# Four weight remainders and the gates of four chunks move to GpSimd in a scan and mixture-of-experts kernel

## The chip, the cores and the metric

The kernel runs on one core of a Trainium2 chip. The metric is the device time of one execution in microseconds (us). The core has five engines with queues of their own: TensorE (PE in the rows; PEld is its weight load), VectorE (DVE), ScalarE (ACT), GpSimd (POOL), and SyncE (SP), which only issues transfers. Each engine takes its instructions in the order in which they were written to its queue, and waits on semaphores of the others.

## The reference

```python
sig = 1.0 / (1.0 + np.exp(-f_logit))          # x, f_logit: 2 x 5056 x 256
f = lower_bound + (1.0 - lower_bound) * sig   # the gate
for t in range(S):
    h = f[:, t] * h + (1.0 - f[:, t]) * x[:, t]
    y[:, t] = h
# two layers over the 10112 tokens of y, 8 experts, w1 256 x 1024, w2 1024 x 256
expert_idx = np.argmax(logits, axis=1)        # layer 0: cosine / tau; layer 1: x @ w_gate
gate_w = probs[np.arange(N), expert_idx]      # softmax of the logits
for e in range(8):
    xe = x[expert_idx == e]
    out[expert_idx == e] = gate_w * (np.maximum(xe @ w1[e], 0.0) @ w2[e])
```

## The kernel before

**The scan.** The tokens come in 40 chunks of 256. For one chunk the inputs are loaded to the tile xf, ScalarE takes a tanh (L495), the gate is made of it by a multiplication and an addition with two columns fa and fb, 256 elements at a time, so twice for a chunk (p_gate, L501 on ScalarE, L212 on GpSimd or VectorE). VectorE then makes the scan's input (one step over 512 elements, L207, from p_scan) and runs two scans (L529). Some chunks later TensorE transposes the result (tile yt, L578 and L580), the row for each token is built (tiles row), the router picks an expert, matmuls into RK count the tokens of each expert (rank_mm L466, L468; rank_up L473, L475), and GpSimd writes the rows to their expert's place in memory with indirect DMAs (X<-row, L714), 128 tokens each.

**Layer 0.** A unit is one tile of 128 sorted tokens with one half of the hidden width. Its tokens are read transposed (xT<-X, issued by SP at L837), TensorE makes the hidden values (hps, L880, 24 matmuls), ScalarE and VectorE make of them an fp16 pair (hT: ScalarE at L893 the rounded part, VectorE at L207 the remainder), and TensorE multiplies by the second weights (ops, L912, 12 matmuls). For the first eight tiles, all with the first half come first (units 0 to 7; ScalarE keeps their partial sums in acc, L916), then the same tiles with the second half (units 8 to 15). Both hps and ops are taken from one set of PSUM buffers, in turn.

**Weights.** Every weight is held as 64 times its value in two fp16 parts: ScalarE writes the rounded part (w_hi, L410), and the remainder is 64 times the source less the rounded part (w_lo). The remainder is one VectorE step over 1024 elements (L207; W<-W,W or W<-ws,W in the rows). For the second half of layer 0 there are 16 such pieces: e 0 to 7 of the first weights (written (0, e) in the diff) and e 0 to 7 of the second weights ((1, e)). The sources of the first weights lie in the tile that later takes the second weights; those of the second weights go through three load buffers (ws), which ScalarE's queue fills again (ws<-w2a) when remainder and rounded part are made. Units 8 and on need all of them.

**Order.** A plan of numbered steps calls these parts; up to step 17 only SP's queue has an order written out, and a scheduler with its own simulated clock orders the others, so a change of cost or engine can move neighbours as well. A remainder can be put behind an instruction already issued (behind in wstep), which is an order only, no data. In the pieces below W_0_ and W_1_ are the first and second half; 102 and 103 are the first weights, 104 and 105 the second ones.

Of the kernel before, what the change touches and what calls it, by code (L numbers as in the profile page):

```python
# [32 lines left out]
 'w0': 10,  # L33
 'wstep0': 0.85,
 'early': 4,
 'gact': (4, 16),
 'urgent': ('scan', 'mm', 'sq', 'pow', 'hi', 'norm', 'top', 'rank', 'rec', 'exp', 'slot', 'up', 'gat', 'put', 'cp'),
 'gdve': 0,
 'wpe': (2, 6, 9, 12),
# [38 lines left out]
        'done': (12, 57)},  # L78
 'hiv': (2,),
 'y1': 'V',  # L80
 'wg': (0, 0, 0, 0),
 'whv': 0,
 'spto': -6,
 'sc': (0, 26),
# [60 lines left out]
def scan_moe_moe_kernel(ctx, tc, xf, emb, cst, tmp, w1a, w2a, w1b, w2b, out, seq, cfg=CFG):  # L145
# [57 lines left out]
    V, A, G, T, SP = nc.vector, nc.scalar, nc.gpsimd, nc.tensor, nc.sync  # L203

    def stt(eng, out, in0, s, in1, op0, op1, **kw):
        assert eng is V
        return eng.scalar_tensor_tensor(out=out, in0=in0, scalar=s, in1=in1, op0=op0, op1=op1, **kw)  # L207

    def ts(eng, out, in0, s1, s2, op0, op1=None):
        if op1 is None:  # L210
            return eng.tensor_scalar(out=out, in0=in0, scalar1=s1, scalar2=None, op0=op0)  # L211
        return eng.tensor_scalar(out=out, in0=in0, scalar1=s1, scalar2=s2, op0=op0, op1=op1)  # L212

    def tt(eng, out, in0, in1, op):
        return eng.tensor_tensor(out=out, in0=in0, in1=in1, op=op)
# [66 lines left out]
    wg = const.tile([P, 2, 2, E], F16, name="wg")  # L282
# [105 lines left out]
    def w_load(item):  # L388
        m, which, h, e = item
        k = 8 * which + e  # L390
        if (m, h) == (0, 0) and k < 8 + cfg["wal"]:
            t = W1[1][:, k % 8].rearrange("p k b f -> p (k b f)").bitcast(F32)
        elif (m, which, h) == (0, 0, 1):
            t = W2[1][:, e].rearrange("p k b d -> p (k b d)").bitcast(F32)
        else:
            t = st.tile([P, 1024], F32, name="ws", tag="ws")
        hwq().dma_start(out=t, in_=wsrc[m][which][:, h, e, :])
        return t

    def w_parts(item, t):  # L400
        m, which, h, e = item
        W = (W2 if which else W1)[h]
        return t.rearrange("p (k f) -> p k f", k=4 if which else 2), W[:, e, :, 0, :], W[:, e, :, 1, :]

    def w_hi(item, t):
        src, hi, lo = w_parts(item, t)
        if item[1] * 8 + item[3] < cfg["whv"] and (item[0], item[2]) == (0, 0):
            ts(V, hi, src, 64.0, None, ALU.mult)
        else:
            A.activation(out=hi, in_=src, func=ACTF.Copy, scale=64.0)  # L410

    def w_lo(item, t):
        src, hi, lo = w_parts(item, t)
        m, which, h, e = item
        k = cfg["wg"][2 * m + h]
        i = 8 * which + e
        on_g = k and (i * k) // 16 != ((i + 1) * k) // 16
        if on_g:
            ts(G, src, src, 64.0, None, ALU.mult)
            tt(G, lo, src, hi, ALU.subtract)  # L420
        else:
            stt(V, lo, src, 64.0, hi, ALU.mult, ALU.subtract)
# [17 lines left out]
    def w_sub(item, t):  # L440

        src, hi, lo = w_parts(item, t)
        k = src.shape[1] // 2
        ps = []
        for i in range(2):
            d = pb.tile([P, 2, 256], F32, name="wd", tag="b").rearrange("p a b -> p (a b)").rearrange("p (k f) -> p k f", k=k)
            T.matmul(out=d, lhsT=idt, rhs=src[:, i * k:(i + 1) * k], start=True, stop=False)
            T.matmul(out=d, lhsT=idn, rhs=hi[:, i * k:(i + 1) * k], start=False, stop=True)
            ps.append(d)
        return ps  # L450

    def w_sub2(item, ps, t):
        src, hi, lo = w_parts(item, t)
        k = src.shape[1] // 2
        for i in range(2):
            A.activation(out=lo[:, i * k:(i + 1) * k], in_=ps[i], func=ACTF.Copy, scale=64.0)
# [269 lines left out]
    tablast = []  # L726
# [492 lines left out]
    def behind(item, eng, other=None):  # L1219
        m, which, h, e = item  # L1220
        if (m, h) == (0, 1):
            u = 2 + e // 2 if which else (e - 2) // 2
            if eng is A and u > 0:
                u -= 1
            if u >= 0:
                other = evs[u][eng is V]
        return tc.issue_after(other) if other is not None else ExitStack()

    def wstep(load, hi, lo, lo2):
        def w_done(item):  # L1230
            assert item[0] or item[2] or now[0] <= 0, "weights too late"
            wdone.add(item)

        if lo2 in wps:
            w_sub2(lo2, *wps.pop(lo2))
            w_done(lo2)
        if lo is not None:
            t = wbuf.pop(lo)
            nlo[0] += 1
            i = nlo[0]  # L1240
            if i in cfg["wpe"]:
                wps[lo] = (w_sub(lo, t), t)
            elif 16 < i <= 32 and tablast:
                with behind(lo, V, tablast[0]):
                    w_lo(lo, t)
                w_done(lo)
            else:
                w_lo(lo, t)
                w_done(lo)
        if hi is not None:  # L1250
            with behind(hi, A):
                w_hi(hi, wbuf[hi])
        if load is not None:
            wbuf[load] = w_load(load)

    def wplan(items, start, step, ahead=0, staged=0):
        x = start

        def it(k):
            return items[k] if 0 <= k < len(items) else None  # L1260

        if ahead:
            for k in range(len(items)):
                at(max(first - 2, int(start + (k - ahead) * step)), cfg["wlp"], wstep, it(k), None, None, None)
        for k in range(len(items) + 4):
            at(int(x), cfg["wprio"], wstep, None if ahead or k < staged else it(k), it(k - 2), it(k - 3), it(k - 4))
            x += step
# [7 lines left out]
    for e in range(E):  # L1275
        at(int(first + cfg["w1s"][0] + e * cfg["w1s"][1]), 60, wstep, (0, 0, 1, e), None, None, None)
# [125 lines left out]
    with ExitStack() as region:  # L1402
# [6 lines left out]
        i = first - 2  # L1409
# [117 lines left out]
```

## Time and profile before

| what | value |
|---|---|
| three runs | 1043.24, 1048.29, 1054.22 us |
| median | 1048.29 us |
| profiled execution | 1049.57 us |
| its span, first to last instruction | 1047.8 us |
[...]
| busy: TensorE, VectorE, ScalarE, GpSimd | 983.6, 780.0, 516.2, 428.2 us |

Durations and starts of single instructions come from the one profiled execution; the median says how fast the kernel usually is. A busy share is a mean over stages that differ, so it has to be read together with the stretches.

### The profile page before, as it was taken

How to read it: one execution, taken by the hardware profiler on the slowest of the kernel's cores; microseconds unless marked ns; L12 is line 12 of the kernel's file. 1: busy time of each engine (PE TensorE's matmuls, PEld its weight loads, DVE VectorE, ACT ScalarE, POOL GpSimd, SP SyncE). 2: the span in 40 equal slices, each digit the busy share in tenths (PEclk: the TensorE clock that was granted, in tenths of full speed). 3: DMA queues.
4: the chain of work that ended last, by engine and by line, in shares of the span. 5: the costliest groups of instructions: out<-in, count | busy, mean ns of one | idle time of the engine just before them, and what ended most of it. 6: DMA issues, size and time to landing. Idle time of an engine off the chain costs nothing.

```text
span 1047.8 us, 33840 instructions
## 1 busy us (share of the span) xinstructions
PE 983.6 (94%) x11795; PEld 859.2 (82%) x11795; DVE 780.0 (74%) x2288; ACT 516.2 (49%) x1266; POOL 428.2 (41%) x686
## 2 busy tenths in 40 slices
PE   5647999998999999999999999999999999999997
PEld 4436899897999899999999888998777777777775
DVE  7878797787888786765448877447777777777775
ACT  6867666555655554665345565443333333333332
POOL 5642447665666565432003550243222222222223
PEclk9967999999999999999999999999999999999999
DMA  9797545887888785965379699652222222221220
GB/s 355 244 328 170 158 93 136 155 163 135 166 161 157 141 150 104 203 200 147 60 181 208 112 212 245 116 104 72 52 52 52 52 52 51 46 52 45 47 47 31
DMA packets 216964, 137.64 MB, mean 131 GB/s; under 512 B 190961, under 2 KB 193918, under 8 KB 216800
## 3 DMA queue, kind: packets, MB, share of 16 engines
q1 hardware_dynamic: 192736, 61.63, 32.1%
q10 hardware_dynamic: 12208, 42.29, 14.7%
q0 software_dynamic: 11856, 31.51, 10.4%
q8 instruction: 105, 1.72, 0.7%
q14 instruction: 59, 0.48, 0.2%
HBM read 58.89 MB, written 38.85 MB: 93 GB/s over the span
## 4 chain that ended last, share of the span: by engine, by line
PE 49%; DMA 3%; DVE 2%; issue 1%; ACT 1%; POOL 0%; ACTq 0%; POOLq 0%
PE hps L869 10%; PE ops L908 10%; PE ops L912 9%; PE hps L880 9%; PE hps L870 5%; PE ops L909 5%; DMA X<-trow,tsl 2%; DMA xT<-X 1%; DVE hT L207 1%; DVE trow L207 0%; DVE W L207 0%; DVE trow L211 0%; PE x2p L978 0%; ACT hT L893 0%; ACT trow L935 0%
## 5 line engine op out<-in xcount | busy, mean ns | idle before, releaser
L880 PE MATMUL hps<-xT,W 128*128 128x128 f16 x4992 | 318.8, 220 | 15.3 <-DMA xT<-X 11.6
L880 PEld LDWEIGHTS <-W 128*128 x4992 | 299.0, 98 | 22.5 <-DMA xT<-X 11.8
L912 PE MATMUL ops<-W,hT 128*128 x2496 | 310.7, 274 | 3.3 <-ACT acc L916 2.7
L912 PEld LDWEIGHTS <-hT 128*128 128x128 f16 x2496 | 234.9, 98 | 31.2 <-issue 4.2
L891 DVE TENSOR_REDUCE acc<-hps 128x256 f32<-128x512 f32 x248 | 169.9, 687 | 63.5 <-PE hps L870 63.5
L207 DVE SCALAR_TENSOR_TENSOR hT<-hps,hT 128x512 f16<-128x512 f32 x208 | 142.0, 686 | 88.7 <-ACT hT L893 87.8
L1083 POOL DMA_INDIRECT out<-osum,ti x83 | 81.1, 977 | 268.7 <-DVE acc L891 227.3
L893 ACT ACTIVATE hT<-acc 128x512 f16<-128x512 f32 x124 | 78.1, 630 | 222.6 <-DVE acc L891 222.6
L893 ACT ACTIVATE hT<-hps 128x512 f16<-128x512 f32 x208 | 123.2, 592 | 116.5 <-PE hps L880 103.1
L869 PE MATMUL hps<-xT,W 128*128 128x256 f16 x992 | 177.1, 273 | 0.0
L870 PE MATMUL hps<-xT,W 128*128 128x128 f16 x992 | 170.4, 219 | 0.0
L908 PE MATMUL ops<-W,hT 128*128 x496 | 167.8, 379 | 0.0
L909 PE MATMUL ops<-W,hT 128*128 x496 | 135.2, 273 | 0.0
L1058 POOL DMA_INDIRECT X<-trow,tsl x83 | 91.8, 1106 | 67.9 <-issue 23.6
L869 PEld LDWEIGHTS <-W 128*128 x992 | 97.1, 98 | 24.1
L714 POOL DMA_INDIRECT X<-row,sl x79 | 90.3, 1143 | 57.3 <-ACT hT L893 19.4
L870 PEld LDWEIGHTS <-W 128*128 x992 | 97.1, 98 | 1.4
L207 DVE SCALAR_TENSOR_TENSOR hT<-acc,hT 128x512 f16<-128x512 f32 x124 | 84.5, 682 | 2.2 <-ACT hT L893 2.2
L908 PEld LDWEIGHTS <-hT 128*128 128x128 f16 x496 | 48.5, 98 | 45.6
L950 ACT ACTIVATE trow<-osum,tsc 128x256 f16<-128x256 f32 x62 | 28.2, 501 | 60.4 <-DVE tsc L212 57.1
L909 PEld LDWEIGHTS <-hT 128*128 128x128 f16 x496 | 48.5, 98 | 4.3
L207 DVE SCALAR_TENSOR_TENSOR W<-ws,W 128x1024 f16<-128x1024 f32 x35 | 42.6, 1221 | 11.8 <-ACT W L410 11.5
(170 smaller groups left out, 1297.1 us busy)
## 6 DMA issues: line engine op xcount, KB each, us to landing
xf<-xf ACTq DMA_DIRECT2D x27, 512.0 KB
ws<-w1b ACTq DMA_DIRECT2D x16, 512.0 KB
ws<-w2b ACTq DMA_DIRECT2D x16, 512.0 KB
W<-w1a SPq DMA_DIRECT2D x11, 512.0 KB
W<-xf SPq DMA_DIRECT2D x8, 512.0 KB
ws<-w2a ACTq DMA_DIRECT2D x8, 512.0 KB
WD<-wq SPq DMA_DIRECT2D x8, 512.0 KB
W<-WD ACTq DMA_DIRECT2D x8, 512.0 KB
```

What stands on the lines that cost most here:

```text
L207: return eng.scalar_tensor_tensor(out=out, in0=in0, scalar=s, in1=in1, op0=op0, op1=op1, **kw)
L714: w = G.indirect_dma_start(out=X[0], out_offset=IndirectOffsetOnAxis(ap=p["sl"][:, i, 0:1], axis=0), in_=p["row"][:, i, :].bitcast(I32), i ...
L869: T.matmul(out=hps[:, c % 2], lhsT=w[2 * k], rhs=xt[:, k:k + 3:2, :], start=(k == 0), stop=False)
L870: T.matmul(out=hps[:, c % 2, 0], lhsT=w[2 * k + 1], rhs=xt[:, k, :], start=False, stop=(k == 1))
L880: T.matmul(out=hps[:, c, :], lhsT=w, rhs=xt[:, a, :], start=(n == 0), stop=(n == 5))
L891: V.tensor_reduce(out=s[:, 2 * c:2 * c + 2].unsqueeze(3), in_=x.rearrange("p c b q -> p c q b"), axis=AX.X, op=ALU.add)
L893: i = A.activation(out=hh[:, 0], in_=hps, func=ACTF.Relu)
L908: T.matmul(out=t["o"].rearrange("p b d -> p (b d)"), lhsT=hT[:, k, :], rhs=w, start=(first and k == 0), stop=False)
L909: T.matmul(out=o, lhsT=hT[:, 4 + k, :], rhs=w[:, 0:D], start=False, stop=(last and k == 3))
L912: T.matmul(out=o, lhsT=hT[:, a + k, :], rhs=w[:, b * D:(b + 1) * D], start=(first and k == 0 and n == 0), stop=(last and k == 3 and n == 2))
L1058: x_write(1, G.indirect_dma_start(out=X[1], out_offset=IndirectOffsetOnAxis(ap=sl[:, i, 0:1], axis=0), in_=d["row"][:, i].bitcast(I32), in ...
L1083: i = ins_of(G.indirect_dma_start(out=out, out_offset=IndirectOffsetOnAxis(ap=ti, axis=0), in_=r, in_offset=None, bounds_check=N - 1, oob_ ...
```

## The change

The gates of chunks 12 to 15 are made by GpSimd in place of ScalarE. Four of the 16 remainders of layer 0's second half are made by GpSimd in two steps, a product with 64 in place over the source and a subtraction of the rounded part, in place of one VectorE step; these four are also not put behind an instruction of VectorE. The old switch wg, which was off everywhere, is gone. Lines after L415 have a number that is smaller by 3 in the new kernel.

```diff
--- before.py
+++ after.py
@@ -33,7 +33,7 @@
  'w0': 10,
  'wstep0': 0.85,
  'early': 4,
- 'gact': (4, 16),
+ 'gact': (4, 12),
  'urgent': ('scan', 'mm', 'sq', 'pow', 'hi', 'norm', 'top', 'rank', 'rec', 'exp', 'slot', 'up', 'gat', 'put', 'cp'),
  'gdve': 0,
  'wpe': (2, 6, 9, 12),
@@ -78,7 +78,7 @@
         'done': (12, 57)},
  'hiv': (2,),
  'y1': 'V',
- 'wg': (0, 0, 0, 0),
+ 'wgs': ((0, 4), (0, 7), (1, 2), (1, 4)),
  'whv': 0,
  'spto': -6,
  'sc': (0, 26),
@@ -412,10 +412,7 @@
     def w_lo(item, t):
         src, hi, lo = w_parts(item, t)
         m, which, h, e = item
-        k = cfg["wg"][2 * m + h]
-        i = 8 * which + e
-        on_g = k and (i * k) // 16 != ((i + 1) * k) // 16
-        if on_g:
+        if (m, h) == (0, 1) and (which, e) in cfg["wgs"]:
             ts(G, src, src, 64.0, None, ALU.mult)
             tt(G, lo, src, hi, ALU.subtract)
         else:
@@ -1241,7 +1238,7 @@
             if i in cfg["wpe"]:
                 wps[lo] = (w_sub(lo, t), t)
             elif 16 < i <= 32 and tablast:
-                with behind(lo, V, tablast[0]):
+                with behind(lo, V, tablast[0]) if (lo[1], lo[3]) not in cfg["wgs"] else ExitStack():
                     w_lo(lo, t)
                 w_done(lo)
             else:
```

GpSimd, from the four indirect writes of chunks 8 and 9 on, before. (inv and ri are small steps of the routers; row<-cs copies token numbers; xf is a gate; the second gate shown here is chunk 16's.)

```order
L714 DMA X_99<-row,sl 82048x258 x4
L212 TENSOR_SCALAR inv<-exr 128x2 x2
L700 COPY row<-cs 128x4
L215 TENSOR_TENSOR ri<-ss,hf 128x4
L211 TENSOR_SCALAR ri<-ri 128x4
L212 TENSOR_SCALAR xf<-xf,fa,fb 128x256 x2
L700 COPY row<-cs 128x4
L215 TENSOR_TENSOR ri<-ss,hf 128x4
L211 TENSOR_SCALAR ri<-ri 128x4
L714 DMA X_99<-row,sl 82048x258 x4
```

The same engine and place, after:

```order
L711 DMA X_99<-row,sl 82048x258 x4
L212 TENSOR_SCALAR xf<-xf,fa,fb 128x256 x2
L212 TENSOR_SCALAR inv<-exr 128x2 x2
L211 TENSOR_SCALAR W_1_105<-W_1_105 128x1024
L697 COPY row<-cs 128x4
L211 TENSOR_SCALAR W_1_105<-W_1_105 128x1024
L215 TENSOR_TENSOR W_1_103<-W_1_105,W_1_103 128x2x512
L211 TENSOR_SCALAR ws<-ws 128x1024
L215 TENSOR_TENSOR W_1_103<-W_1_105,W_1_103 128x2x512
L212 TENSOR_SCALAR xf<-xf,fa,fb 128x256 x4
L215 TENSOR_TENSOR ri<-ss,hf 128x4
L215 TENSOR_TENSOR W_1_105<-ws,W_1_105 128x4x256
```

Chunk 12's two gates now stand right behind the writes. Three products, two subtractions and the gates of chunks 13 and 14 stand ahead of the first small step ri, and more follow.

VectorE, from the input of chunk 12 (xf, 128x512) and its scans on, before:

```order
L207 SCALAR_TENSOR_TENSOR xf<-xf 128x512
L529 SCALAR_TENSOR_TENSOR xf<-xf 128x256 x2
L207 SCALAR_TENSOR_TENSOR hT<-hps,hT 128x512
L207 SCALAR_TENSOR_TENSOR W_1_103<-W_1_105,W_1_103 128x2x512 x2
L207 SCALAR_TENSOR_TENSOR hT<-hps,hT 128x512
L207 SCALAR_TENSOR_TENSOR W_1_103<-W_1_105,W_1_103 128x2x512 x2
L207 SCALAR_TENSOR_TENSOR hT<-hps,hT 128x512
L207 SCALAR_TENSOR_TENSOR W_1_103<-W_1_105,W_1_103 128x2x512 x2
L207 SCALAR_TENSOR_TENSOR W_1_105<-ws,W_1_105 128x4x256 x2
L212 TENSOR_SCALAR pi<-ss 128x2
L207 SCALAR_TENSOR_TENSOR hT<-hps,hT 128x512
```

The same engine and place, after:

```order
L207 SCALAR_TENSOR_TENSOR xf<-xf 128x512
L526 SCALAR_TENSOR_TENSOR xf<-xf 128x256 x2
L207 SCALAR_TENSOR_TENSOR hT<-hps,hT 128x512
L207 SCALAR_TENSOR_TENSOR W_1_103<-W_1_105,W_1_103 128x2x512 x2
L207 SCALAR_TENSOR_TENSOR hT<-hps,hT 128x512
L207 SCALAR_TENSOR_TENSOR W_1_103<-W_1_105,W_1_103 128x2x512
L207 SCALAR_TENSOR_TENSOR hT<-hps,hT 128x512
L207 SCALAR_TENSOR_TENSOR W_1_103<-W_1_105,W_1_103 128x2x512
L207 SCALAR_TENSOR_TENSOR W_1_105<-ws,W_1_105 128x4x256 x2
L212 TENSOR_SCALAR pi<-ss 128x2
L207 SCALAR_TENSOR_TENSOR hT<-hps,hT 128x512 x2
```

The input and the scans of chunk 12 have kept their place ahead of the steps hT of units 0 to 4, and two of the remainders between these are gone.

TensorE, at the second group of rank matmuls (tri16b) of chunks 10 and 11, before. It stands behind the second matmul of unit 5 (ops) and ahead of unit 9's hps:

```order
L912 MATMUL ops<-W_0_104,hT 128x256
L473 LDWEIGHTS tri16b
L473 MATMUL RK<-oh,tri16b 128x32
L475 LDWEIGHTS ones_109
L475 MATMUL RK<-oh,ones_109 128x24
L475 LDWEIGHTS ones_109
L475 MATMUL RK<-oh,ones_109 128x16
L475 LDWEIGHTS ones_109
L475 MATMUL RK<-oh,ones_109 128x8
L811 REGISTER_ALU
L880 LDWEIGHTS W_1_103
L880 MATMUL hps<-xT,W_1_103 128x128
```

The same group of rank matmuls, after; the rows ahead of it are unit 7's hps, and those behind it the second matmul of unit 4:

```order
L877 MATMUL hps<-xT,W_0_102 128x128
L470 LDWEIGHTS tri16b
L470 MATMUL RK<-oh,tri16b 128x32
L472 LDWEIGHTS ones_109
L472 MATMUL RK<-oh,ones_109 128x24
L472 LDWEIGHTS ones_109
L472 MATMUL RK<-oh,ones_109 128x16
L472 LDWEIGHTS ones_109
L472 MATMUL RK<-oh,ones_109 128x8
L909 LDWEIGHTS hT
L808 REGISTER_ALU
L909 MATMUL ops<-W_0_104,hT 128x256
```

The group has moved ahead by more than one unit, so that the second matmuls of units 4 and 5 now stand behind it.

## Rows read from the trace of the kernel before

**Rows 1.** The page, busy time of TensorE, its share of the span and its instructions.
```profile
PE 983.6 (94%) x11795; PEld 859.2 (82%) x11795; DVE 780.0 (74%) x2288; ACT 516.2 (49%) x1266; POOL 428.2 (41%) x686
```

**Rows 2.** Stretches of 10 us: busy us (instructions) by engine, clock, DMA share, GB/s.
```profile
80.00:90.00 10.00, 5.22 (x55) 4.50 (x54) 8.83 (x10) 8.75 (x17) 3.00 (x4) 0.83 0.94 170
90.00:100.00 10.00, 7.84 (x61) 6.97 (x59) 6.79 (x14) 6.89 (x17) 1.43 (x2) 0.66 0.66 180
...
120.00:130.00 10.00, 9.85 (x117) 8.90 (x117) 6.40 (x36) 5.86 (x22) 7.80 (x10) 1.00 0.74 186
```

**Rows 3.** Timeline of TensorE: start, us, line, operation, [idle before <-releaser].
```profile
82.28 1.59 PE L912 MATMUL ops<-W,hT 128*128 x12
88.56 2.74 PE L880 MATMUL hps<-xT,W 128*128 128x128 f16 x24 [4.70 <-DMA xT<-X]
...
93.41 2.72 PE L912 MATMUL ops<-W,hT 128*128 x12
...
100.31 2.72 PE L912 MATMUL ops<-W,hT 128*128 x12 [2.47 <-ACT acc L916]
...
107.36 1.86 PE L880 MATMUL hps<-xT,W 128*128 128x128 f16 x24
109.08 1.56 PE L912 MATMUL ops<-W,hT 128*128 x12
...
147.83 1.39 PE L880 MATMUL hps<-xT,W 128*128 128x128 f16 x22
```

**Rows 4.** Timeline of VectorE from 76 to 92 us.
```profile
76.69 0.69 DVE L207 SCALAR_TENSOR_TENSOR xf<-xf 128x512 f32<-128x512 f32 x1 [1.07 <-ACT xf L501]
...
85.70 0.69 DVE L207 SCALAR_TENSOR_TENSOR hT<-hps,hT 128x512 f16<-128x512 f32 x1 [1.17 <-ACT hT L893]
...
90.91 0.68 DVE L207 SCALAR_TENSOR_TENSOR hT<-hps,hT 128x512 f16<-128x512 f32 x1
```

**Rows 5.** Timeline of GpSimd from 79 to 120 us.
```profile
79.89 1.48 POOL L714 DMA_INDIRECT X<-row,sl  x1 [0.30 <-issue]
...
113.77 1.45 POOL L212 TENSOR_SCALAR xf<-xf,fa,fb 128x256 f32<-128x256 f32 x2 [16.89 <-ACT xf L495]
...
118.11 1.42 POOL L714 DMA_INDIRECT X<-row,sl  x1 [0.72 <-DVE mx L648]
```

**Rows 6.** Timeline of ScalarE from 75 to 101 us; ACTq is its DMA queue.
```profile
75.56 1.09 ACT L501 ACTIVATE xf<-xf,fb,fa 128x256 f32<-128x256 f32 x2
...
93.66 0.33 ACTq L397 DMA_DIRECT2D ws<-w2a  x1
...
97.26 1.06 ACT L410 ACTIVATE W<-ws 128x1024 f16<-128x1024 f32 x1 [1.92 <-DMA ws<-w2a]
...
99.88 0.38 ACT L916 ACTIVATE acc<-ops 128x256 f32<-128x256 f32 x1
```

**Rows 7.** Groups by shape: count | busy us, mean ns of one | idle before, releasers.
```profile
L212 POOL TENSOR_SCALAR xf<-xf,fa,fb 128x256 f32<-128x256 f32 x46 | 25.7, 565 | 37.5 <-ACT xf L495 37.5
...
L212 POOL TENSOR_SCALAR inv<-exr 128x2 f32<-128x2 f32 x41 | 12.4, 302 | 3.2 <-DMA exr<-X 0.3
L215 POOL TENSOR_TENSOR tsh<-tsh,lf 128x16 f32<-128x16 f32 x41 | 10.5, 256 | 5.5 <-DVE ter L207 3.0 <-DVE tse L1036 0.9
L215 POOL TENSOR_TENSOR lf<-exr,us 128x2 f32<-128x2 f32 x41 | 9.3, 226 | 93.1 <-DVE us L211 51.6 <-DVE tm L1015 17.1 <-DVE tse L207 16.3
L215 POOL TENSOR_TENSOR trow<-tse,lf 128x2 f32<-128x2 f32 x41 | 8.9, 216 | 19.3 <-DVE tse L1040 14.3 <-DVEq L1380 3.2 <-DVE tmx L1006 0.6
...
L207 DVE SCALAR_TENSOR_TENSOR W<-ws,W 128x1024 f16<-128x1024 f32 x35 | 42.6, 1221 | 11.8 <-ACT W L410 11.5
```

**Rows 8.** Timelines of GpSimd (POOL) and VectorE (DVE) where both work.
```profile
12.86 2.42 POOL L212 TENSOR_SCALAR W<-W,fa,fb 128x256 f32<-128x256 f32 x2
...
113.89 0.96 DVE L529 TENSOR_TENSOR_SCAN xf<-xf 128x256 f32<-128x256 f32 x1
...
115.32 0.74 DVE L529 TENSOR_TENSOR_SCAN xf<-xf 128x256 f32<-128x256 f32 x1
```

## Prediction

> **What bounds the kernel now.** I read the busy shares first, then the same shares by stretches of 10 us, then the timelines of the engines where those stretches show idle time on TensorE, and last the mean durations by shape. The busy shares name TensorE as the bound, with 94% of the span [rows 1]. The stretches show that this is not true everywhere: between 80 and 90 us TensorE is busy 5.22 us of 10, between 90 and 100 us 7.84, and from 120 us on it is nearly full (9.85) [rows 2]. Both moved kinds of work, the gates of chunks 12 to 15 and the four remainders, lie between 75 and 115 us, so they lie where TensorE still waits. After that it has no idle time with which to catch up, so **a shift of TensorE at about 110 us is a shift of the end**. I therefore ask one question only: when does TensorE start the second matmul of unit 4 (109.08 us now [rows 3])?
>
> In that stretch the timeline of TensorE has two long waits: 4.70 us before 88.56 for a load of tokens, and 2.47 us before 100.31 for an accumulation by ScalarE [rows 3]. VectorE is full there (8.83 of 10 us between 80 and 90 [rows 2]), but TensorE does not wait for it. GpSimd is busy 3.00 us between 80 and 90, 1.43 between 90 and 100 [rows 2], and then idle until 113.77 [rows 5].
>
> **What the change removes.** Four remainders at 1.22 us [rows 7] leave VectorE: 4.9 us. Eight gates leave ScalarE, 1.09 us for each two as at 75.56 [rows 6]: 4.4 us. Neither engine is the bound, so by itself this is worth nothing; it counts by what comes earlier behind it.
>
> **What it adds on GpSimd.** A gate takes 0.565 us, a 128x2 operation of the same kind 0.302 [rows 7], so an element costs 263/254 = 1.04 ns. The product in place over 1024 elements is then 0.302 + 1022 x 0.00104 = 1.36 us. A subtraction with two tensors of 1024 elements has no row. From 128x2 (226 ns) and 128x16 (256 ns) [rows 7] an element costs 30/14 = 2.1 ns, and 1024 of them 0.226 + 1022 x 0.0021 = 2.4 us. Those sizes are small, so I bound it: not below the product's 1.36, and with the whole spread of the small rows (216 to 256 ns would give 2.9 ns) not much above 3.2. I take 2.4, from the row with the same two-tensor form. Four pairs are 15.0 us (10.9 to 18.2), eight gates 4.5 us: 19.5 us, in 7.0 + 8.6 + 13.8 = 29.4 us that are idle between 80 and 113.77. They fit. [...]
>
> **What it moves: the gate of chunk 12.** On GpSimd it stands behind four indirect writes (the order of GpSimd shows it), the last of which ends at 79.89 + 1.48 = 81.37 [rows 5]. With two gates at 2 x 0.565 us [rows 7] it ends at 82.5; on ScalarE it ended at 75.56 + 1.09 = 76.65 [rows 6]. VectorE has kept its place for chunk 12's input (76.69 [rows 4], the order of VectorE), ahead of the hidden-layer steps of all these units, so it stands still for about 5.8 us. What hides this: the step of unit 0, and with it the second matmul of unit 0 (82.28), slips to about 85.2, but TensorE then waits until 88.56 for tokens anyway [rows 3]. The next that can be late is the second matmul of unit 1 at 93.41, which needs a PSUM buffer that VectorE's step for unit 3 frees. Now this step ends at 90.91 + 0.68 = 91.59, which is 14.9 us after 76.69 [rows 4]. Two remainders before it are gone (2.44 us), and the idle 1.17 us before 85.70 [rows 4] closes up: 11.3 us. So it ends at 82.5 + 11.3 = 93.8, **0.4 us late** at most if nothing else holds VectorE.
>
> **What else holds VectorE: GpSimd itself.** Both work at once in [rows 8]. Two gates of GpSimd, 1.13 us by the mean of their form [rows 7], took 2.42 us at 12.86, beside VectorE's scans and inputs; and the scan at 113.89, beside two gates, took 0.96 us where the next took 0.74. The 0.22 us are most of the 0.26 us that 256 elements take at 1.04 ns. So an operation of VectorE with two inputs in SBUF waits out the data of a GpSimd operation, and the other way round. [...]
>
> By rows alone: between 82.5 and the step of unit 3 GpSimd runs about three products and two subtractions. Their data take 3 x 1.06 + 2 x 2.15 = 7.5 us. VectorE's steps from hps have one input in SBUF and I count them as free of it; they are 4 x 0.68 of 11.3 us, about a quarter. So VectorE loses 0.75 x 7.5 = 5.6 us if each collision costs the full data time, and nothing if none does. With 0.22 of 0.26, 85%, it is 4.8 us. The second matmul of unit 1 then starts at 93.8 + 4.8 = 98.6, **5.2 us late**.
>
> **What TensorE gets back.** The second matmul of unit 2 waited 2.47 us for ScalarE's accumulation of unit 1 [rows 3, 6], which ended at 99.88 + 0.38; it stood behind a weight conversion at 97.26 that had waited 1.92 us for its load. In the new order this matmul uses another PSUM buffer, freed by a VectorE step that is done in time (it stands right behind the step of unit 4). So 2.47 us go, and 5.2 becomes 2.7 at unit 4.
>
> **What takes its place.** The rank matmuls of chunks 10 and 11 now stand ahead of the second matmul of unit 4 (the order of TensorE shows it), and they wait for a VectorE step that is queued behind a chain of weight loads. These loads, which rotated through three buffers, now follow each other in one buffer for three of them, since GpSimd still holds another. One link takes from issue (93.66) to conversion (97.26) 3.6 us [rows 6], then 1.06 for the conversion and 1.22 for the remainder. From a conversion at 97.26: remainder done 99.6, next load's conversion 103.3 to 104.4, remainder 105.6, scans of chunk 14 (2 x 0.74) 107.1, hidden step of unit 6 107.8, rank step 108.0, two groups of rank matmuls 108.5. Unit 4 would start at **108.5, 0.6 us early** instead of 2.5. With VectorE held, the first link starts later: its buffer is freed by the remainder just ahead of the step of unit 3, so by the same 4.8 us less the slack that ScalarE's issue now has (93.66 against a remainder that ends at 90.9: 2.7 us, of which the 93.8 - 91.6 = 2.2 us of lateness take most). That is 108.5 + 4.3 = 112.8, **3.7 us late**. It is later than the 2.7 of the paragraph above, so it decides.
>
> **The sum.** Profiled execution 1049.57 us (span 1047.8); plus 3.7 is 1053.3. Its time lies 1.28 us above the median of the three runs, 1048.29, so on the scale of that median 1052.0. I forecast **1052 us**. Terms bounded below: without any collision 1048.29 - 0.6 = 1047.7; with a subtraction of 3.2 us and full collisions VectorE loses 0.75 x (3.2 + 2 x 3.0) = 6.9 instead of 4.8, 1054.1.
>
> Costed at nothing: the later indirect writes of chunks 10 and 11 (from 118.11 [rows 5]), because TensorE comes to the tokens of the next table only at 147.83 [rows 3], and three or four us are a small part of that; the remainder of the last GpSimd item, which I put at 116 to 118 and which the second matmul of unit 8 needs, four units of 1.86 + 1.56 us [rows 3] and more after 109.08, so not before 122.8. If the cover were gone, each would cost its lateness. The weight sources are multiplied in place; the two in the layer's other buffer and the two in load buffers are not read again.
>
> **Rivals.**
> (a) No collisions worth the name: the 0.96 against 0.74 is one pair of rows, and the steps could interleave better at 1024 elements. Then 1047.7 to 1049; nothing is to be seen.
> [...]
> (c) Clearly slower. GpSimd's own chain grows so late that chunk 13's gates, which stand behind three products and two subtractions, hold VectorE's input of chunk 13, with the step of unit 5 behind it. TensorE needs that step at 107.36 [rows 3]. The gates end at 82.5 + 0.5 + 1.1 (a copy) + 3 x 1.36 + 2 x 2.4 + 1.1 = 94.1, at 102 if every operation waits out a remainder of 1.2 us. It decides only from about 106, that is from a subtraction of 4.5 us on. At 8 us the gates end near 113, the step of unit 5 1.4 us later, 114.4 against 107.36, and unit 4 stands 7 us late, behind which the last subtraction is late for unit 8 by some 5 us more: 1048.3 + 12 = 1060.
> (d) The change does not do what it says: the order shows the four pairs on GpSimd, so I give this nothing.
>
> **How the numbers follow.** Forecast 0.5 (1050 to 1055); (a) 0.28; (b) 0.1; (c) 0.12. A change of 1%, 10.5 us, is about what a measurement here tells from none: the runs lie between 1043.24 and 1054.22. Faster by over 1% (below 1037.8) needs twice the gain of (b): 0.03. Slower by over 1% (above 1058.8) is (c) with a little over: 0.1. The rest, 0.87, is within 1%. The range leaves out the far end of (c) and the best of (b): 1044 to 1058.
>
> **What would show it.** In the new profile: VectorE idle some 5.8 us before chunk 12's input with GpSimd's gate as releaser; the second matmul of unit 1 at 97 to 100 us and released by VectorE's hidden step; no wait of unit 2's second matmul on ScalarE; unit 4's second matmul at 111 to 114 us behind a wait of the rank matmuls; GpSimd's products 1.4 to 2.6 us, its subtractions 2.4 to 3.6 us; VectorE's remainders beside them above 1.22. I am wrong if the remainders stay at 1.22 beside GpSimd (then (a)), if the subtraction takes 4.5 us or more (then (c)), or if TensorE is shifted after 120 us by something that I cost at nothing.

## The result and the profile after

The changed kernel took 1057.74 us in the median of 13 runs (1053.19 to 1063.65), the kernel before 1049.92 us in 13 runs beside it. The ratio is 1.0078, with a 95% interval of 1.0054 to 1.0101: some 8 us slower. The forecast was 3.7 us slower (1052 us). The profiled execution took 1057.16 us, with a span of 1055.4.

Up to the second matmul of unit 4 the profile after goes much as forecast. TensorE's timeline, as in [rows 3] (second matmuls of units 0, 1 and 2, unit 7's hps, the rank matmuls, the second matmul of unit 4):

```profile
85.16 2.17 PE L909 MATMUL ops<-W,hT 128*128 x12 [2.05 <-DVE hT L207]
...
97.23 2.71 PE L909 MATMUL ops<-W,hT 128*128 x12 [1.93 <-DVE hT L207]
...
102.30 1.80 PE L909 MATMUL ops<-W,hT 128*128 x12
...
107.89 1.50 PE L877 MATMUL hps<-xT,W 128*128 128x128 f16 x24
111.97 0.18 PE L470 MATMUL RK<-oh,tri16b 128*128 128x32 f16 x1 [2.57 <-DVE er L215]
...
112.07 1.79 PE L909 MATMUL ops<-W,hT 128*128 x12
```

The 4.70 us wait for tokens and the 2.47 us wait for ScalarE of [rows 3] are gone. In their place the second matmul of unit 1 waits for VectorE's hidden step and starts at 97.23, 3.8 us later than at 93.41; unit 2's starts 2.0 us later; the rank matmuls wait 2.57 us for VectorE (er), and unit 4's starts at 112.07, **3.0 us later** than at 109.08. VectorE, in answer to [rows 4]:

```profile
82.40 0.69 DVE L207 SCALAR_TENSOR_TENSOR xf<-xf 128x512 f32<-128x512 f32 x1 [5.98 <-POOL xf L212]
...
85.03 2.54 DVE L207 SCALAR_TENSOR_TENSOR W<-W,W 128x1024 f16<-128x1024 f32 x2
...
88.09 1.61 DVE L207 SCALAR_TENSOR_TENSOR W<-W,W 128x1024 f16<-128x1024 f32 x1
...
91.36 5.12 DVE L207 SCALAR_TENSOR_TENSOR W<-ws,W 128x1024 f16<-128x1024 f32 x2
...
96.46 1.50 DVE L207 SCALAR_TENSOR_TENSOR hT<-hps,hT 128x512 f16<-128x512 f32 x2
97.88 1.37 DVE L212 TENSOR_SCALAR sc<-pi 128x2 int32<-128x2 int32 x1
...
103.27 2.86 DVE L207 SCALAR_TENSOR_TENSOR xf<-xf 128x512 f32<-128x512 f32 x1
```

It waits 5.98 us for chunk 12's gate. Then two remainders take 5.12 us where two in [rows 7] take 2.44, and the input of chunk 13 takes 2.86 us instead of 0.69. What stands beside them on GpSimd (TENSOR_SCALAR over 1024 elements is a product, TENSOR_TENSOR a subtraction):

```profile
81.27 1.10 POOL L212 TENSOR_SCALAR xf<-xf,fa,fb 128x256 f32<-128x256 f32 x2
...
83.98 3.14 POOL L211 TENSOR_SCALAR W<-W 128x1024 f32<-128x1024 f32 x1
...
87.59 2.77 POOL L211 TENSOR_SCALAR W<-W 128x1024 f32<-128x1024 f32 x1
90.33 3.08 POOL L215 TENSOR_TENSOR W<-W,W 128x1024 f16<-128x1024 f32 x1
93.39 3.74 POOL L211 TENSOR_SCALAR ws<-ws 128x1024 f32<-128x1024 f32 x1
97.10 2.12 POOL L215 TENSOR_TENSOR W<-W,W 128x1024 f16<-128x1024 f32 x1
...
103.46 2.12 POOL L215 TENSOR_TENSOR W<-ws,W 128x1024 f16<-128x1024 f32 x1
105.56 3.21 POOL L211 TENSOR_SCALAR ws<-ws 128x1024 f32<-128x1024 f32 x1
...
114.77 2.12 POOL L215 TENSOR_TENSOR W<-ws,W 128x1024 f16<-128x1024 f32 x1
```

The products take 2.77 to 3.74 us, the subtractions 2.12 to 3.08.

The lateness of unit 4 is no chance of this pair of profiles. The same matmul in the kernel before run again and in the changed kernel run again (below, on other chips; in the second case with the rank matmuls that it stands behind):

```profile
104.98 1.56 PE L912 MATMUL ops<-W,hT 128*128 x12
```

```profile
109.98 0.18 PE L470 MATMUL RK<-oh,tri16b 128*128 128x32 f16 x1 [3.27 <-DVE er L215]
...
110.09 2.72 PE L909 MATMUL ops<-W,hT 128*128 x12
```

In all seven traces of the kernel before (the experiments below included, with empty instructions or later hints) it starts between 104.98 and 109.08 us, in the mean at 106.6. In six traces of the changed kernel it starts between 109.38 and 112.07, in the mean at 110.2, each time behind a wait of the rank matmuls for VectorE, of 2.57 to 5.84 us. That is 3.6 us later. (A seventh, with 125 empty instructions, is later by these: 113.37.)

Much later TensorE is still late: the second matmul that starts at 461.42 before starts at 466.07 after, 4.65 us later. And right behind that comes a stop of nearly the whole core: from 470 to 472 us after, TensorE, ScalarE and GpSimd are busy for 0.00 us and VectorE for 0.24. First the kernel before, then the one after:

```profile
461.42 1.48 PE L912 MATMUL ops<-W,hT 128*128 x12
462.73 1.50 PE L880 MATMUL hps<-xT,W 128*128 128x128 f16 x24
464.53 0.61 PE L978 MATMUL x2p<-id,trow 128*128 128x128 f16 x8 [0.30 <-PEq L1380]
464.98 1.47 PE L912 MATMUL ops<-W,hT 128*128 x12
...
466.34 1.50 PE L880 MATMUL hps<-xT,W 128*128 128x128 f16 x24
467.68 1.47 PE L912 MATMUL ops<-W,hT 128*128 x12
```

```profile
466.07 1.47 PE L909 MATMUL ops<-W,hT 128*128 x12
467.38 1.50 PE L877 MATMUL hps<-xT,W 128*128 128x128 f16 x24
473.27 1.01 PE L975 MATMUL x2p<-id,trow 128*128 128x128 f16 x8 [4.39 <-PEq L1377]
474.07 2.77 PE L909 MATMUL ops<-W,hT 128*128 x12
...
476.74 2.29 PE L877 MATMUL hps<-xT,W 128*128 128x128 f16 x24
478.86 1.47 PE L909 MATMUL ops<-W,hT 128*128 x12
```

Before, TensorE passes from layer 0's full tables to the rest with 0.30 us of waiting; after, it waits 4.39 us for its own sequencer (PEq), at the line of the test whether the tail tables of layer 0 hold anything (last_tiles; they hold nothing here). Behind the wait the matmuls run slowly: 2.77 us for the second matmul against 1.47, 2.29 for the next hps against 1.50. The stretches of 10 us from 470 on, before and after, give the granted clock in the column ahead of the last two: 1.00 against 0.66. In the second stretch it is 0.50 from 472 to 478 us, behind the stop, and 1.00 again from 480 to 482.

```profile
470.00:480.00 10.00, 10.00 (x146) 9.50 (x144) 7.09 (x24) 6.38 (x15) 2.18 (x7) 1.00 0.41 109
```

```profile
470.00:480.00 10.00, 6.73 (x57) 5.90 (x58) 1.00 (x5) 2.37 (x6) 1.26 (x2) 0.66 0.31 70
```

At 478.86 against 467.68 TensorE is 11.18 us late, 6.5 more than ahead of the stop. Some 3.6 us are regained by the end (7.6 us between the spans). The branch instruction itself, before and after (count, then minimum, median and maximum in ns, and its start):

```profile
L1380 PEldq COMPARE_BRANCH  x1: 424/424/424, 463.5 to 463.5; - x1
```

```profile
L1377 PEldq COMPARE_BRANCH  x1: 4790/4790/4790, 468.2 to 468.2; - x1
```

It is the same instruction with the same outcome, 0.42 us before and 4.79 us after. No line of the change is near it: the engines run hand-ordered code there that both kernels share. While it stands, queue 8, one of the two of the kind "instruction" in the profile (the other is queue 14), moves one packet (packets, MB, share of 16 engines; the stretch from 470.4 to 473.0 us). In the whole span it moves 1.74 MB in 106 packets, 16.4 KB each:

```profile
q8 instruction: 1, 0.02, 2.7%
```

That packet by itself does not set the two kernels apart. The kernel before moves one as well around its quick branch, from 461 to 466 us; it comes between 465 and 466, when TensorE has already gone on (464.53):

```profile
q8 instruction: 1, 0.02, 1.4%
```

The second test of this kind, at the end of layer 1, takes 3.4 us in both kernels.

### The profile page after: what moved, and what is told of

Its sections match the earlier page's. It is cut to its first block, busy times and chain, and to the rows that moved or that the text cites. A ratio compares the mean times of both kernels' runs of the same rounds, so it can differ in the third digit from the quotient of the medians.

```text
span 1055.4 us, 33854 instructions
## 1 busy us (share of the span) xinstructions
PE 987.1 (94%) x11795; PEld 862.8 (82%) x11795; DVE 785.7 (74%) x2284; ACT 512.0 (49%) x1258; POOL 452.8 (43%) x702
## 3 DMA queue, kind: packets, MB, share of 16 engines
q8 instruction: 106, 1.74, 0.7%
## 5 line engine op out<-in xcount | busy, mean ns | idle before, releaser
L1055 POOL DMA_INDIRECT X<-trow,tsl x83 | 89.6, 1080 | 76.0 <-issue 26.9
L215 POOL TENSOR_TENSOR lf<-exr,us 128x2 f32<-128x2 f32 (+1 forms) x42 | 9.3, 223 | 97.4 <-DVE us L211 52.9
```

The source lines that it names most:

```text
L1055: x_write(1, G.indirect_dma_start(out=X[1], out_offset=IndirectOffsetOnAxis(ap=sl[:, i, 0:1], axis=0), in_=d["row"][:, i].bitcast(I32), in ...
```

## The experiments

**The change's two parts, and chunk 12's gate.** The gates alone ('wgs' emptied), the remainders alone, the change with chunk 12's gate left on ScalarE, and the changed kernel once more:

```diff
e1_gates  - 'wgs': ((0, 4), (0, 7), (1, 2), (1, 4)),   + 'wgs': (),
e2_rem    - 'gact': (4, 12),                           + 'gact': (4, 16),
e3_g13    - 'gact': (4, 12),                           + 'gact': (4, 13),
```

Gates alone: 

> The gates of chunks 12 to 15 by GpSimd, all 16 remainders by VectorE. Collision theory (the price is GpSimd's products and subtractions, which hold VectorE): ratio 0.999 to 1.003; VectorE idles some 6 us ahead of chunk 12's input as in the changed kernel, but its remainders between 82 and 97 us stay at 1.2 us each, and the second matmul of unit 4 starts at most 2 us later than the 109.08 us of before. Gate theory (the price is VectorE's wait for chunk 12's gate): ratio 1.006 to 1.009, the whole loss. Order theory (the price is the rank matmuls ahead of unit 4, waiting for weight loads in series): ratio 0.999 to 1.002, since they do not stand there in this kernel.

Remainders alone: 

> The four remainders by GpSimd, the gates of chunks 12 to 15 by ScalarE as before. Collision theory: ratio 1.003 to 1.008; GpSimd's products 2.5 to 3.7 us and its subtractions 2 to 3 us, two or three VectorE operations lengthened by 1 to 2.5 us each between 82 and 112 us, the second matmul of unit 4 1 to 3 us late. Gate theory: ratio 0.996 to 1.001, no loss without the gates. Order theory: ratio 1.004 to 1.008, with a wait of 2 us or more of the rank matmuls ahead of unit 4, even where VectorE's operations are not lengthened.

Chunk 12's gate back: 

> The changed kernel with only chunk 12's gate back on ScalarE. Collision theory: ratio 1.003 to 1.007, VectorE does not wait ahead of chunk 12's input but is lengthened later, unit 4 at 110 to 112 us. Gate theory: ratio 0.998 to 1.002, since the 6 us wait is gone. Order theory: ratio 1.004 to 1.008.

Again: 

> The changed kernel once more, for a second profile. If the loss beyond unit 4 (3.0 us late there, 7.6 us at the end) is the program's, the second profile shows TensorE's sequencer waiting some 4 us at about 469 us again and the same lateness at the end. If it is chance, that wait is 0.3 us as in the kernel before, and the span is shorter by about 4 us.

Measured, against the kernel before on the same chip (chips differ, 1066.7 us for the kernel before here, so only ratios of one chip are compared): 1.0105 (1.0055 to 1.0154), 1.0072 (1.0045 to 1.0098) and 1.0099 (1.0064 to 1.0133); the changed kernel once more took 1078.03 us. No theory fits all three: each part alone costs about what the whole costs, though the gates alone have no product on GpSimd, and the remainders alone have no late gate. What the four have in common is the branch: 4.1, 4.2, 4.0 and 4.4 us. So the long branch is no chance of one execution.

Unit 4's second matmul starts at 111.80 us with the gates alone and at 110.48 with the remainders alone, so either part alone makes it late. With chunk 12's gate back it starts at 107.64, inside the range of the kernel before and not at the 110 to 112 expected, and the kernel is as slow as the others.

The rows of the two parts still show both mechanisms. With the gates alone, VectorE waits 4.85 us for chunk 12's gate, its remainders take 2.35 us in pairs as ever, and it is GpSimd that loses, with 6.80 us for four gates (2.26 us by the mean of [rows 7]):

```profile
80.35 0.69 DVE L207 SCALAR_TENSOR_TENSOR xf<-xf 128x512 f32<-128x512 f32 x1 [4.85 <-POOL xf L212]
...
88.70 2.35 DVE L207 SCALAR_TENSOR_TENSOR W<-W,W 128x1024 f16<-128x1024 f32 x2
90.97 2.35 DVE L207 SCALAR_TENSOR_TENSOR W<-ws,W 128x1024 f16<-128x1024 f32 x2
```

```profile
90.21 6.80 POOL L212 TENSOR_SCALAR xf<-xf,fa,fb 128x256 f32<-128x256 f32 x4 [7.42 <-ACT xf L492]
```

With the remainders alone, chunk 12's input starts at 75.85 as before, and two remainders with a subtraction between them take 4.28 us; the product behind the subtraction takes 3.74:

```profile
75.85 0.69 DVE L207 SCALAR_TENSOR_TENSOR xf<-xf 128x512 f32<-128x512 f32 x1 [1.06 <-issue]
...
87.35 4.28 DVE L207 SCALAR_TENSOR_TENSOR W<-ws,W 128x1024 f16<-128x1024 f32 x2
```

```profile
88.06 2.49 POOL L215 TENSOR_TENSOR W<-W,W 128x1024 f16<-128x1024 f32 x1
90.53 3.74 POOL L211 TENSOR_SCALAR ws<-ws 128x1024 f32<-128x1024 f32 x1
```

**The place of the branch.** The branch is TensorE's 11802nd instruction before, and the 11805th after, because three more semaphore waits stand ahead of it. To move it without the change, empty instructions were put at the start of TensorE's program:

```diff
+    for _ in range(3):
+        nc.tensor.nop(hint='pad', nofuse=True)
     with _tile.TileContext(nc, schedule_with_timeline_sim=True) as tc:
```

The kernel before, unpadded: 

> The kernel before once more, for a profile on this chip. Position theory (the branch at the end of layer 0's full tables is quick or slow by where it stands in TensorE's program): TensorE's compare-and-branch takes some 0.4 us here again, as in the first profile. Chance theory (the branch is slow in some executions of any kernel): as likely 4 us as 0.4.

The kernel before with three: 

> The kernel before with three empty instructions put at the very start of TensorE's program, where it idles for microseconds; the rest is the same, instruction by instruction. The branch now is the 11805th of TensorE's instructions, as in the changed kernel. Position theory: TensorE's compare-and-branch takes 4 to 5 us, ratio 1.004 to 1.008, with nothing of the change in it. Rival (the loss is the change's own): 0.4 us and ratio 0.998 to 1.002.

The changed kernel with 125: 

> The changed kernel with 125 empty instructions at the start of TensorE's program, so that the branch moves by 128 against the kernel before. Position theory: if this place is a good one, TensorE's compare-and-branch takes 0.4 us and the ratio falls to 1.000 to 1.004, the change's own part; if it is not a good one, 4 us as in the changed kernel. Rival: ratio 1.006 to 1.010 whatever the place.

Unpadded, the branch took 0.424 us again. **With three empty instructions and nothing of the change it took 4.29 us**, and the timeline shows the same stop:

```profile
L1380 PEldq COMPARE_BRANCH  x1: 4290/4290/4290, 464.6 to 464.6; - x1
```

```profile
463.81 1.50 PE L880 MATMUL hps<-xT,W 128*128 128x128 f16 x24
469.30 1.01 PE L978 MATMUL x2p<-id,trow 128*128 128x128 f16 x8 [3.98 <-PEq L1380]
470.10 2.57 PE L912 MATMUL ops<-W,hT 128*128 x12
```

The ratio was 1.0104 (1.0054 to 1.0154). With 125, the changed kernel's branch is short, but TensorE stops 2.28 us a little later, after seven matmuls, and the ratio stayed at 1.0104 (1.006 to 1.0148):

```profile
L1377 PEldq COMPARE_BRANCH  x1: 580/580/580, 470.2 to 470.2; - x1
```

```profile
471.64 0.93 PE L909 MATMUL ops<-W,hT 128*128 x7
474.85 1.23 PE L909 MATMUL ops<-W,hT 128*128 x5 [2.28 <-issue]
```

The stop has moved, not gone. (The ratio expected for a good place, 1.000 to 1.004, did not come. The 125 cost TensorE 9.9 us at its very start, where it waits in any case; the first matmul that it waits for came at 10.08 us instead of 6.66, and unit 4's second matmul stands at 113.37, 3.2 us behind the mean of the other traces of the changed kernel. So this ratio holds a part of that.)

**Equal places.** Four kernels on one chip, two with the branch at the 11805th and two at the 11866th place:

> The kernel before with three empty instructions ahead, again, to stand beside the changed kernel on one chip with the branch at the same place (11805th) in both. Position theory: ratio 1.004 to 1.010, within 0.3% of the changed kernel's. Collision theory as the prediction had it (the change's own part is all of the loss): 0.998 to 1.002.

> The changed kernel. Ratio 1.005 to 1.010 as measured. If the change's own part is the forecast's 3.7 us, it stands 0.35% above the padded kernel before; if the lateness of unit 4 is regained by the end, no more than 0.1% above it.

> The kernel before with 64 empty instructions at the start: branch at the 11866th. Position theory: the two branches take either some 0.5 us or 3.5 to 4.8 us each, by place alone; ratio 1.000 plus 0.5% for a slow first branch, less 0.3% for a quick second one. Rival: ratio 1.000 and the first branch at 0.4 us.

> The changed kernel with 61 empty instructions, so that both branches stand at the same places as in the kernel before with 64. Position theory: the two branches take the same time as there, within 0.5 us; the difference of the two ratios is the change's own part, 0 to 0.4%.

Measured: before with three 1.0055 (1.002 to 1.009), changed 1.0077 (1.0048 to 1.0105); before with 64 1.0039 (1.0005 to 1.0073), changed with 61 1.0058 (1.0028 to 1.0088). The first branch took 3.9 and 4.2 us at the one place, 2.4 and 2.0 at the other; the second 3.4 and 3.7 against 0.47 and 0.47. The branches go with the place, whichever kernel it is. What is left between the kernels is 0.2% in either pair, which is within the intervals.

The quick second branch gained nothing. In every trace the program ends 8.7 to 9.1 us after the start of the second branch, whether that takes 3.1 to 3.9 us or 0.47, so the 0.3% expected for it is not there; only the first branch costs.

**The hint.** Ahead of each branch the program gives TensorE a hint of it, 813 instructions ahead of the first. It was put five steps later, 366 ahead, with the places of the branches kept:

```diff
-    at(last0 + cfg["t0at"][0] - 9, 39, lambda: read_count(0))
+    at(last0 + cfg["t0at"][0] - 4, 39, lambda: read_count(0))
-    at(NU - 9, 39, lambda: read_count(1))
+    at(NU - 4, 39, lambda: read_count(1))
```

In the kernel before: 

> The kernel before, with the two prefetch hints of TensorE's branches (and the reading of the counts that they need) put five steps later in the plan: the first hint 366 instructions ahead of its branch instead of 813, the branches at the places that they had. If a slow branch comes of a hint that stands too far ahead for the place, the second branch falls from 3.4 to about 0.5 us and the first stays at 0.4: ratio 0.994 to 0.998, faster than both kernels. If the hint's distance does not matter, 0.4 and 3.4 us as before and ratio 0.998 to 1.002.

In the changed one: 

> The changed kernel with the same later hints. If the distance matters, its first branch falls from 4.2 to 4.8 us to about 0.5 us and the second from 3.5 to 0.5: ratio 0.996 to 1.000, and the difference to the other kernel of this pair is the change's own part, 0.1 to 0.4%. If it does not matter, 4 and 3.5 us and ratio 1.005 to 1.010.

Measured 1.0009 (0.9974 to 1.0045) and 1.0108 (1.0068 to 1.0149). In the kernel before the branches stayed at 0.43 and 3.41 us; in the changed one the first fell to 2.54 us and the second stayed at 3.6:

```profile
L1377 PEldq COMPARE_BRANCH  x1: 2544/2544/2544, 487.6 to 487.6; - x1
```

At this place the branch took 3.9 to 4.8 us in eight traces with the early hint. So the distance seems to have a part in it, by one execution; it does not make the branch short, and no version that beats both kernels came of it. The two ratios differ by 0.99%, some 10 us, where the first branches differ by only 2.1 us.

**The parts at equal branch.** The padded kernel before, the change, and its parts, on one chip, all with the long branch:

> The kernel before with three empty instructions ahead: the slow branch without any of the change. Ratio 1.004 to 1.010; it is the base against which the next three are read, which all have the slow branch.

> The changed kernel. If the change's own part is the forecast's 3.7 us: 0.35% above the padded kernel before. If its lateness is regained after the tables: within 0.1% of it.

> The gates alone on GpSimd. Its branch is slow too. Collision theory: within 0.1% of the padded kernel before; gate theory: 0.3 to 0.5% above it, as much as the whole change.

> The remainders alone on GpSimd. Its branch is slow too. Collision theory: 0.2 to 0.4% above the padded kernel before; gate theory: within 0.1% of it.

Measured 1.0023 (0.9991 to 1.0056), 1.0111 (1.0073 to 1.0149), 1.0100 (1.0062 to 1.0139) and 1.0086 (1.0058 to 1.0114); the first branch took 4.1, 4.1, 4.5 and 4.4 us. Here the change stands 0.88% above the padded kernel, more than in the two pairs before. Each part alone stands above it as well, by 0.8 and 0.6% (by the medians the three are 0.6, 0.4 and 0.4%), so neither theory of a single part holds, and the parts do not add up. Unit 4's second matmul is late with either part too: it starts at 112.56 us with the gates alone, 111.06 with the remainders alone, 109.68 with both, 107.83 in the padded kernel.

## Why the prediction was wrong

**The step that failed** is the one in bold in the first part: "a shift of TensorE at about 110 us is a shift of the end". I asked for nothing behind unit 4, because both kernels run the same code there. They do, but not from the same place in the program: where TensorE's program is longer by three instructions, the branch at 463 to 468 us takes some 4 us in place of 0.42, and this term was not in the sum at all. That the place is the cause of the long branch, and that it costs time, is shown by the kernel before with three empty instructions: the branch from 0.42 to 4.29 us, the 12 matmuls behind it 2.57 instead of 1.47, and a ratio of 1.0104, 1.0055 and 1.0023 in three measurements (the interval of the last holds 1), 1.0061 or 6.4 us in the mean. The claim that no idle time follows rested on one stretch, 120 to 130 us; no timeline behind 150 us is among the rows, and the stop lies far behind it. Why 11802 is a good place and 11803 (the gates alone), 11805 and 11807 (the remainders alone) are not, is open. A stop that shrinks with the padding (4.3, 2.4 and 0.6 us at 3, 64 and 128 places on), and that comes back seven matmuls later (2.28 us), made me suspect a wait for one of queue 8's packets of 16.4 KB. These traces do not show such a wait: the kernel before moves one packet there as well, and its branch with the same outcome takes 0.42 us.

**The change's own part** was of the right size where the forecast worked it out: unit 4 was to be 3.7 us late, and it is 3.6 us late in the mean of the traces. What of it is left at the end is less well known. The three pairs at equal places give 0.22, 0.19 and 0.88%, in the mean 0.43% or 4.5 us, with intervals on each ratio of 0.3 to 0.4% either way, so that the first two differences are not clear of zero. Of the third, the traces do not show where it comes from: the branch starts at 486.3 us in the one and at 486.5 in the other. The pair with the later hints points to more as well. The sum of the mean and the branch's 6.4 us is 10.9, against the 8 to 12 us of the three timed comparisons of the change (1.0078, 1.0077, 1.0111); two of these are in both, so it is no check of its own.

Point by point:
- Chunk 12's gate: VectorE waits 5.98 us, forecast 5.8. That unit 0 hides it was right; the 4.70 us wait for tokens that hid it is gone.
- Collisions: shown on the rows of both engines (5.12 us for two remainders against 2.44, 3.08 us for the subtraction beside them against 2.12), so that rival (a) is out; with the gates alone, where GpSimd has no products, the remainders keep their 2.35 us in pairs. I had VectorE lose 4.8 us ahead of unit 3's step. It lost 0.2 + 0.4 + 2.8 us on the remainders at 85.03, 88.09 and 91.36, 3.4 us, so unit 1's second matmul came at 97.23 and not 98.6.
- Product and subtraction held VectorE differently. The remainders that started inside the products at 83.98 and 87.59 lost 0.2 and 0.4 us, less than the 1.06 us of data that I gave a product. VectorE's steps from hps, which I counted as free, took 0.67 to 0.68 us at 84.44, 87.49 and 89.62, beside the same products, against 0.686 in the mean of the kernel before. The subtractions took from VectorE about what I gave them (2.15 us): the input of chunk 13 lost 2.2 us beside the one at 103.46.
- Which of the two engines loses is not the same in all rows. With the gates alone GpSimd lost 4.5 us on four gates and VectorE nothing; at 103.46 the subtraction took 2.12 us, as short as any, and it was VectorE that lost 2.2.
- GpSimd's prices: the products were mis-sized, 1.36 us forecast and 2.77 to 3.74 measured; no product ran with VectorE idle, so what of it is waiting is not known. The least in ten traces is 2.77, beside different steps of VectorE. The subtractions were near, 2.4 and 2.12 to 3.08. The four pairs took 22.3 us instead of 15.0.
- The 2.47 us wait for ScalarE went, as forecast. The rank matmuls took its place with a wait of 2.57 us; unit 4 started 3.0 us late, forecast 3.7.
- Costed at nothing and right: the later indirect writes and the last remainder. Unit 8's second matmul is 4.0 us late, 1.0 more than unit 4's, after waits of about half a microsecond for VectorE.
- Rival (c) did not come about: chunk 13's gates ended at 101.38, ahead of the 106 from which they would decide. A gain, to which the forecast gave 0.1 as (b), did not come about either: unit 4 is late in every trace of the changed kernel.
- Single profiles of one kernel differ by some 4 us at unit 4 (105 us in the kernel before run again, 109.08 in the first), so the 3.0 us of one pair of executions say little; the means over all traces and the timed ratios are what carries the size.

## What to carry to other kernels

Where a program has a branch, look at what the branch itself takes in both kernels: on TensorE it hung here on the branch's place in the program (0.42 us at the 11802nd, 3.9 to 4.8 at the 11805th), and an edit that adds instructions ahead of it, were it only three waits, moves that place. So pad the kernel before to the same place before a difference of 1% is put down to an edit, or the edit is thrown away. And work moved from a full VectorE to an idle GpSimd was not free of VectorE here (two remainders took 5.12 us beside it, against 2.44): read what both engines' operations take while they overlap, not alone.

## What was not expected of the hardware

A branch of TensorE took 0.42 to 4.79 us with one outcome, by its place in the program and, in one execution, by the distance of its hint; behind the stop the granted clock was lower (0.66 against 1.00 from 470 to 480 us, 0.50 from 472 to 478), and the next 12 matmuls took 2.77 us against 1.47. Beside GpSimd an operation of VectorE with a single small input was slow as well: a step over 128x2 elements (sc<-pi) that takes 0.16 us took 1.37 us at 97.88, beside a subtraction. And a product over 1024 elements with one input took GpSimd longer (2.77 to 3.74 us in the changed kernel) than a subtraction with two (2.12 to 3.08), both beside a busy VectorE.
